# Linear-attention denominators: replicated by one matmul per group of heads, or made head-wise on 32-column array tiles and spread by DMA

## The chip, the cores and the metric

The kernel runs on one core of a Trainium2 chip. The time is the device time of one execution in microseconds, median over executions. All runs compared here are of the fast state (e6, a single look, counts as unknown), at a mean granted TensorE clock of 0.98 to 1.00, and each experiment ran beside the kernel before on the same chip. A profile is one execution; its span (first to last instruction) is 1.7 us shorter than its time (521.8 against 523.49 us before).

TensorE does the matmuls. VectorE, ScalarE and GpSimd are called DVE, ACT and POOL in the profile. SyncE (SP) issues nearly all DMA here; SPq is its sequencer. PEld is TensorE's weight load.

## The reference

For 2048 tokens of width 576 the kernel computes `x + attention(layernorm(x)) + geglu(layernorm(x))`. The attention is linear, with 32 heads of 18 columns:

```python
pq, pk = phi(q), phi(k)
kv = jnp.einsum("bhsd,bhse->bhde", pk, v)
z = jnp.einsum("bhsd->bhd", pk)
num = jnp.einsum("bhqd,bhde->bhqe", pq, kv)
den = jnp.einsum("bhqd,bhd->bhq", pq, z)[..., None] + 1e-6
o = num / den                      # one denominator per token and head
# ... then @ wo; and (gelu(x @ w_gate) * (x @ w_up)) @ w_down
```

## The kernel before

The 2048 tokens are worked in four chunks of 512. After an attention part at the start (to about 71 us), each token chunk has a gate/up phase of 18 blocks (matmuls on 64-row tiles in pairs) and a down phase of 4 token tiles with 2 half tiles each. A half tile is 36 matmuls of the down projection and 5 of the attention, summed in one PSUM bank (PSUM is the memory in which TensorE sums).

The features of the heads lie in five groups: four of 7 heads (126 rows) and one of 4 heads (72 rows). `pqT` holds the query features. The division is done by scaling `pqT` before the attention matmuls. The kernel before makes each denominator already replicated 18 times, with a block-masked `zrep` of 126 columns, so one matmul gives the denominators of one group in the layout of `pqT`:

```python
def den_mm(sc, c, bank):
    rows = DH * HCH[c]
    ps = ps_all[:rows, bank, :]
    nc.tensor.matmul(ps, lhsT=zrep[:rows, c, :rows], rhs=pqT[:rows, c, sc * SC:(sc + 1) * SC], start=True, stop=True)
    den_evac(sc, c, ps)               # VectorE: + eps, to SBUF
# ... den_norm: 128-column reciprocals on VectorE, then pqT *= d on GpSimd
# ... first token chunk: three row-paired units (12 matmuls) in gate/up blocks 2, 3 and 4
# ... later token chunks: one den_mm in each of 4 or 5 half tiles of the down phase before
```

Weights come three blocks ahead, on SP's queue, which waits for a free buffer (88.1 us in 67 waits in the profile before):

```python
if blk > 0:
    load_gu(blk + NWBUF - 1, i)       # NWBUF = 4, nc.sync.dma_start, waits until a buffer is free
```

And the two row tiles of a gate/up unit take turns on a bank through an empty instruction on another engine, GpSimd except in the very first block. That instruction stands in GpSimd's program order, so the second half of a unit waits for everything GpSimd has before it (1.39 us in e1 below):

```python
self.turn = self.relay.nop()          # relay: nc.gpsimd, or nc.sync for the first block
```

Of the kernel before, what the change touches and what calls it, by code (L numbers as in the profile page):

```python
# [39 lines left out]
TD = 4  # L40
XW = 640
PKW = 580


class _Ring:
# [11 lines left out]
def kernel(  # L57
# [68 lines left out]
    make_identity(nc, ident[:])  # L126
    eps_ln = const.tile([P, 1], F32, name="eps_ln")
    nc.vector.memset(eps_ln[:], EPS_LN)
    eps_att = const.tile([P, 1], F32, name="eps_att")
    nc.vector.memset(eps_att[:], EPS_ATT)  # L130

    def spin(count):

# [6 lines left out]
    pqT = persist.tile([P, NCH, S], BF16, name="pqT")  # L140
    wo2 = persist.tile([P, NCH, D], BF16, name="wo2")
    m_sb = persist.tile([P, NCH, D], BF16, name="m_sb")
    zrep = persist.tile([P, NCH, CR], BF16, name="zrep")
    kvT = persist.tile([P, NCH, CR], BF16, name="kvT")

    nc.vector.memset(pqT[HP:P, NCH - 1, 0:2 * SC], 0.0)
    nc.vector.memset(zrep[HP:P, NCH - 1, :], 0.0)

    def load_wo():
        nc.sync.dma_start(wo2[:CR, 0:4, :], A_wo[0:4 * CR, :].rearrange("(c p) j -> p c j", p=CR))  # L150
# [49 lines left out]
    nc.gpsimd.memset(g_sb[0:HP, 4, HALF:D], 0.0)  # L200
    nc.gpsimd.memset(g_sb[HP:P, 4, 0:HALF], 0.0)

    ZQ = 32
    z_ones = const.tile([P, ZQ], BF16, name="z_ones")
    nc.gpsimd.memset(z_ones[:], 1.0)
    z_sb = apool.tile([P, D], BF16, name="z_sb")
    nc.gpsimd.memset(z_sb[:], 0.0)
    zsel = const.tile([P, CR], BF16, name="zsel")
    nc.gpsimd.memset(zsel[:], 0.0)
    for g in range(P // ZQ):  # L210
        nc.gpsimd.memset(zsel[g * ZQ:g * ZQ + 1, :], 1.0)
# [249 lines left out]
        rows = DH * HCH[c]  # L461
        return ps_all[:rows, b4, c * CR:c * CR + rows] if c < 4 else ps_all[:rows, b1, 0:rows]

    def z_stage(b4, b1):
        for c in range(NCH):
            rows = DH * HCH[c]
            nc.tensor.matmul(
                chunk_out(c, b4, b1), lhsT=z_sb[:, c * CR:c * CR + rows], rhs=zsel[:, :rows],
                start=(c in (0, 4)), stop=True, skip_group_check=True,
            )  # L470
        mask_pair(zrep, b4, b1)

    def kv_stage(b4, b1):
        for kt in range(KT):
# [6 lines left out]
                )  # L481
        mask_pair(kvT, b4, b1)

    den_sb = {}

    def den_evac(sc, c, ps):
        rows = DH * HCH[c]
        d = dwork.tile([P, SC], F32, name="den_sb", tag="den_sb", bufs=6)
        nc.vector.tensor_scalar_add(out=d[:rows, :], in0=ps, scalar1=EPS_ATT)
        den_sb[sc, c] = d  # L490

    def den_mm(sc, c, bank):
        rows = DH * HCH[c]
        ps = ps_all[:rows, bank, :]
        nc.tensor.matmul(ps, lhsT=zrep[:rows, c, :rows], rhs=pqT[:rows, c, sc * SC:(sc + 1) * SC], start=True, stop=True)  # L495
        den_evac(sc, c, ps)

    def den_pair(items, outs):

        rows = DH * HCH[items[0][1]]  # L500

        def part(r):

            return slice(r.start, min(r.stop, P if rows <= P - HP + 8 else rows))

        return _Unit(
            outs,
            lambda i, r, kt: zrep[part(r), items[i][1], :rows],
            lambda i, r, kt: pqT[part(r), items[i][1], items[i][0] * SC:(items[i][0] + 1) * SC],
            nc.sync, first=(0,), then=(0,),  # L510
        )

    def den_norm(sc, c, q, pieces):
        w = SC // pieces
        rows = DH * HCH[c]
        d = den_sb[sc, c][:rows, q * w:(q + 1) * w]
        cols = slice(sc * SC + q * w, sc * SC + (q + 1) * w)
        for h in range(0, w, P):
            nc.vector.reciprocal(out=d[:, h:h + P], in_=d[:, h:h + P])  # L519

        def scale():
            nc.gpsimd.tensor_tensor(out=pqT[:rows, c, cols], in0=pqT[:rows, c, cols], in1=d, op=ALU.mult)  # L522
        return scale



# [84 lines left out]
    g_copy(1, (3, 288), [(ALL, 3, 0, 288, 288, nc.scalar), (ALL, 2, 0, 0, 288, nc.vector)])  # L611
    for _, step, n in todo[tail:]:
        step(n)
    q_unit(12)
    for step in (q_exp1, q_min, q_max):
        step(12)
    g_last(0)
    z_sums(1)
    g_copy(3, (6, 288), [(ALL, 6, 0, 288, 288, nc.scalar), (ALL, 5, 0, 0, 288, nc.vector)])
    g_copy(4, (0, 288), [(HI, 0, 0, 288, 288, nc.scalar), (LO, 0, 0, 0, 288, nc.vector)])  # L620
    z_copies(1)
    q_unit(13)
    z_stage(2, 3)
    kv_stage(6, 5)
    for step in (q_exp1, q_min, q_max):
        step(13)


    q_banks = _Ring(list(range(6)))
    prev = None  # L630
    for units in [[15, 16], [17, 18], [14, 19], None]:
        if units:
            u = q_pair(units)
            u.p1()
        if prev:
            prev[1].p2()
            for step in (q_exp1, q_min, q_max):
                for i in prev[0]:
                    step(i)
        prev = (units, u)  # L640
    scales = []
    den_jobs = [(0, c, q, 2) for c in range(NCH) for q in range(2)]

    asmall_cm.__exit__(None, None, None)
    awork_cm.__exit__(None, None, None)
# [9 lines left out]
            nc.sync.dma_start(wd_sb[:, f0:f0 + WDS, :], wd_view[:, f0:f0 + WDS, :])  # L655
            wd_loaded[0] += WDS


    DEN_FROM = 2
    DEN_PAIRS = [[(0, 0), (0, 1)], [(0, 2), (0, 3)], [(0, 4), (1, 4)]]  # L660

    def gu_pair(sc, k):
        cs = slice(sc * SC, (sc + 1) * SC)
        blk = sc * (NF // GUB) + k
        wg, wu, wr = gu_blocks.pop(blk)
        units = []
        for i in range(GUB):
            b = [banks.next(), banks.next()]
            fcol = slice(i * P, (i + 1) * P)

            def lhs(a, rows, kt, fcol=fcol):
                if kt == 4:
                    return wr[rows, fcol]
                return (wg, wu)[a][rows, kt, fcol]

            u = _Unit([ps_all[:, b[0], :], ps_all[:, b[1], :]], lhs, lambda a, rows, kt: xnT[rows, kt, cs],
                      nc.sync if blk == 0 else nc.gpsimd)
            if blk > 0:
                load_gu(blk + NWBUF - 1, i)
            u.p1()  # L680
            units.append((b, u))
        if sc == 0 and k == 1:
            load_wo()
        elif sc == 0 and k >= 2:
            load_wd_slice()
        den = None
        if sc == 0 and 0 <= k - DEN_FROM < len(DEN_PAIRS):
            items = DEN_PAIRS[k - DEN_FROM]
            den = den_pair(items, [ps_all[:DH * HCH[c], banks.next(), :] for _, c in items])
            den.p1()  # L690
        for i, (b, u) in enumerate(units):
            u.p2()
            gl = fwork.tile([P, SC], F32, name="gl")
            nc.scalar.activation(out=gl[:], in_=ps_all[:, b[0], :], func=ACT.Gelu_apprx_tanh)  # L694
            nc.vector.tensor_tensor(out=hT[:, GUB * k + i, :], in0=ps_all[:, b[1], :], in1=gl[:], op=ALU.mult)  # L695
        if den:
            den.p2()
            for (dsc, c), ps in zip(items, den.outs):
                den_evac(dsc, c, ps)

    def m_stage(c, acc_bank):
        rows = DH * HCH[c]
        for hf in range(2):
            b = (acc_bank + 2 + (2 * c + hf) % 6) % 8
            hs = slice(hf * HALF, (hf + 1) * HALF)
            nc.tensor.matmul(  # L706
                ps_all[:rows, b, :HALF], lhsT=kvT[:rows, c, :rows], rhs=wo2[:rows, c, hs], start=True, stop=True,
            )
            nc.scalar.copy(out=m_sb[:rows, c, hs], in_=ps_all[:rows, b, :HALF])

    def down_tile(sc, j, hooks):
        n = sc * TPC + j
# [3 lines left out]
        for hf in range(2):  # L716
            hs = slice(hf * HALF, (hf + 1) * HALF)
            todo = hooks.pop(0) if hooks else {}
            acc_bank = banks.next()
            acc = ps_all[:, acc_bank, :HALF]  # L720
            for f in range(NF):
                if f in todo:
                    todo[f](acc_bank)
                nc.tensor.matmul(  # L724
                    acc, lhsT=hT[:, f, j * P:(j + 1) * P], rhs=wd_sb[:, f, hs], start=(f == 0), stop=False,
                )
            for c in range(NCH):
                rows = DH * HCH[c]
                nc.tensor.matmul(  # L729
                    acc, lhsT=pqT[:rows, c, ts_], rhs=m_sb[:rows, c, hs], start=False, stop=(c == NCH - 1),  # L730
                )
            nc.vector.tensor_tensor(out=res[:, hs], in0=acc, in1=x_sb[:, n, hs], op=ALU.add)  # L732
            if last:
                nc.sync.dma_start(out_view[:, n, hs], res[:, hs])
        if not last:
            nc.sync.dma_start(out_view[:, n, :], res[:])

    for sc in range(NSC):
        for k in range(NF // GUB):
            gu_pair(sc, k)  # L740
            if scales:
                scales.pop(0)()
            if den_jobs and k > DEN_FROM:
                scales.append(den_norm(*den_jobs.pop(0)))
        while wd_loaded[0] < NF:
            load_wd_slice()

        hooks = [{6 * c_: (lambda b, c_=c_: m_stage(c_, b)) for c_ in range(NCH)} if sc == 0 else {}]
        if sc + 1 < NSC:
            for c_ in range(NCH):  # L750
                def dn(b, c=c_, nsc=sc + 1):
                    if (nsc, c) not in den_sb:
                        den_mm(nsc, c, (b + 2) % 8)
                    den_norm(nsc, c, 0, 1)()
                hooks.append({0: dn})
        for j in range(TPC):
            down_tile(sc, j, hooks)

# [29 lines left out]
```

## Time and profile before

| | before |
|---|---|
| time, median of the first 3 runs | 524.03 us (523.87 to 524.6) |
| span of the profiled run | 521.8 us |
| TensorE busy | 516.3 us |
| VectorE busy | 251.2 us, of which reciprocals 68.3 |
| a gate/up phase without denominators | 70.03 us (18 blocks of 3.89) |
| down phases 1 to 3, with denominators | 42.5, 41.4, 41.4 us |

The row of a group on the profile's page reads: line, engine and operation, tiles, shapes, count, then busy us and the mean ns of one, then the engine's idle time ahead of them and what ended it. These two rows are the work that the change shrinks and moves:

```profile
L519 DVE RECIPROCAL den_sb<-den_sb 126x128 f32<-126x128 f32 (+1 forms) x80 | 68.3, 910 | 0.5
...
L522 POOL TENSOR_TENSOR pqT<-pqT,den_sb 126x512 bf16<-126x512 bf16 (+3 forms) x25 | 24.1, 965 | 317.0 <-DVE den_sb L519 282.4
```

GpSimd's 317 us of idle time cost nothing: it is not on the chain that ended last, of which TensorE is 96%.

### The profile page before, as it was taken

The page shows a single profiled execution, that of the slowest core. Times are in us where ns is not written, and L with a number is a line of the kernel's source. Part 1 is how long each engine was busy: PE and PEld are TensorE (multiplying, and loading weights), DVE is VectorE, ACT ScalarE, POOL GpSimd, SP SyncE. Part 2 cuts the span into 40 slices and gives each one's busy share as a digit, 9 for nine tenths or more (in the row PEclk, how much of TensorE's full clock was granted, in tenths as well). Part 3 has the DMA queues.
Part 4 walks back from the last instruction along what each step waited for, and adds up shares of the span by engine and source line. Part 5 has one row for each costly group of instructions (what it writes and reads, how often), then busy time and mean ns, then how long its engine had stood idle before and what let it go on. Part 6 is the DMA issues. An engine that isn't in the chain of part 4 may idle for free.

```text
span 521.8 us, 10779 instructions
## 1 busy us (share of the span) xinstructions
PE 516.3 (99%) x4562; PEld 313.8 (60%) x4562; DVE 251.2 (48%) x438; ACT 143.8 (28%) x296; POOL 36.4 (7%) x62
## 2 busy tenths in 40 slices
PE   8999999999999999999999999999999999999997
PEld 7777755555587754444577644444777544445775
DVE  7996565876358323433388033333584233333100
ACT  6899442322320013323200032332000123322000
POOL 3011000211001100000012000000011000000000
PEclk9999999999999999999999999999999999999999
DMA  8434509898500045455300155555000355540000
GB/s 267 75 62 122 155 27 264 238 287 258 162 13 13 11 126 158 142 159 157 92 13 13 43 163 152 158 147 157 26 25 13 105 159 158 142 133 1 13 13 23
DMA packets 106362, 57.96 MB, mean 111 GB/s; under 512 B 13386, under 2 KB 105802, under 8 KB 106314
## 3 DMA queue, kind: packets, MB, share of 16 engines
q1 hardware_dynamic: 105706, 56.62, 38.8%
q8 instruction: 35, 0.57, 0.5%
q10 hardware_dynamic: 608, 0.66, 0.4%
q14 instruction: 13, 0.11, 0.1%
HBM read 52.94 MB, written 2.36 MB: 106 GB/s over the span
## 4 chain that ended last, share of the span: by engine, by line
PE 96%; ACT 1%; DMA 1%; DVE 1%; issue 0%; ACTq 0%
PE ps_all L358 55%; PE ps_all L724 27%; PE ps_all L729 4%; PE ps_all L259 3%; PE ps_all L303 3%; PE ps_all L387 3%; DMA wqkv_sb<-in_A_wqkv_dram 1%; PE ps_all L495 1%; PE ps_all L477 0%; PE ps_all L706 0%; ACT xnT L248 0%; ACT L116 0%; DVE g_sb L597 0%; ACT phi_e L279 0%; ACT z_sb L335 0%; DVE pqT L447 0%
## 5 line engine op out<-in xcount | busy, mean ns | idle before, releaser
L358 PE MATMUL ps_all<-xnT,wg 64*128 64x512 bf16 x1152 | 272.7, 376 | 0.0
L358 PE MATMUL ps_all<-xnT,wu 64*128 64x512 bf16 x1152 | 271.8, 376 | 0.0
L695 DVE TENSOR_TENSOR hT<-ps_all,gl 128x512 bf16<-128x512 f32 x144 | 99.4, 691 | 162.0 <-ACT gl L694 161.3
L694 ACT ACTIVATE gl<-ps_all 128x512 f32<-128x512 f32 x144 | 86.0, 597 | 314.4 <-PE ps_all L358 295.0
L358 PEld LDWEIGHTS <-wu 64*128 64x128 bf16 x1152 | 108.3, 94 | 66.2
L358 PEld LDWEIGHTS <-wg 64*128 64x128 bf16 x1152 | 108.3, 94 | 66.0
L724 PE MATMUL ps_all<-wd_sb,hT 128*128 128x288 bf16 x1152 | 147.0, 286 | 0.0
L724 PEld LDWEIGHTS <-hT 128*128 128x128 bf16 x1152 | 112.3, 98 | 30.7 <-issue 1.3
L519 DVE RECIPROCAL den_sb<-den_sb 126x128 f32<-126x128 f32 (+1 forms) x80 | 68.3, 910 | 0.5
L732 DVE TENSOR_TENSOR res<-ps_all,x_sb 128x288 bf16<-128x288 f32 x32 | 14.6, 457 | 88.0 <-PE ps_all L729 88.0
L358 PE MATMUL ps_all<-xnT,wr 64*128 64x512 bf16 x288 | 55.2, 376 | 0.0
L522 POOL TENSOR_TENSOR pqT<-pqT,den_sb 126x512 bf16<-126x512 bf16 (+3 forms) x25 | 24.1, 965 | 317.0 <-DVE den_sb L519 282.4
L729 PE MATMUL ps_all<-m_sb,pqT 126*128 126x288 bf16 (+1 forms) x160 | 24.9, 286 | 0.0
L358 PEld LDWEIGHTS <-wr 64*128 64x128 bf16 x288 | 14.5, 94 | 16.8 <-issue 0.7
L259 PE MATMUL ps_all<-wqkv_sb,xnT 128*128 128x288 bf16 x160 | 22.5, 286 | 0.6 <-DMA wqkv_sb<-in_A_wqkv_dram 0.5
L259 PEld LDWEIGHTS <-xnT 128*128 128x128 bf16 x160 | 15.3, 98 | 6.7 <-issue 0.8
L303 PE MATMUL ps_all<-hT,xn 128*128 128x288 bf16 (+4 forms) x144 | 18.2, 273 | 0.0
L729 PEld LDWEIGHTS <-pqT 126*128 126x128 bf16 (+1 forms) x160 | 15.5, 97 | 4.1
L387 PE MATMUL ps_all<-xnT,wqkv_sb 128*126 128x512 bf16 (+1 forms) x70 | 17.4, 379 | 0.0
L303 PEld LDWEIGHTS <-xn 128*128 128x128 bf16 x144 | 13.9, 98 | 3.3
L287 DVE SCALAR_TENSOR_TENSOR hT<-ps_all,phi_e 128x288 bf16<-128x288 f32 x32 | 13.2, 449 | 4.4 <-ACT phi_e L283 3.8
L279 ACT ACTIVATE phi_e<-ps_all 128x288 f32<-128x288 f32 x32 | 12.9, 409 | 3.4 <-PE ps_all L259 1.9
(78 smaller groups left out, 184.7 us busy)
## 6 DMA issues: line engine op xcount, KB each, us to landing
wg<-in_B_w_gate_dram SPq DMA_DIRECT2D x72, 256.0 KB, 2.8
wu<-in_B_w_up_dram SPq DMA_DIRECT2D x72, 256.0 KB, 3.5
wd_sb<-in_B_w_down_dram SPq DMA_DIRECT2D x12, 432.0 KB, 4.5
wr<-in_B_w_gate_dram SPq DMA_DIRECT2D x72, 32.0 KB, 2.6
wr<-in_B_w_up_dram SPq DMA_DIRECT2D x72, 32.0 KB, 3.0
out_dram<-res SPq DMA_DIRECT2D x15, 144.0 KB, 1.8
x_sb<-in_A_x_dram SPq DMA_DIRECT2D x3, 576.0 KB, 7.4
wqkv_sb<-in_A_wqkv_dram SPq DMA_DIRECT2D x2, 576.0 KB
```

The source lines that it names most:

```text
L259: nc.tensor.matmul(ps_all[:, k_bank(n, hf), :HALF], lhsT=xnT[:, kt, n * P:(n + 1) * P], rhs=wqkv_sb[:, kt, D + hf * HALF:D + (hf + 1) * HALF],
L287: nc.vector.scalar_tensor_tensor(out=out_, in0=ps, scalar=0.0, in1=e, op0=ALU.max, op1=ALU.add)
L303: nc.tensor.matmul(ps_all[:, b, col:col + w], lhsT=xn[:, n, kt * P:(kt + 1) * P], rhs=pk[:, n, p0:p0 + w], start=(n == 0 and col == 0), st ...
L358: return nc.tensor.matmul(self.outs[i], lhsT=self.lhs(i, rows, kt), rhs=self.rhs(i, rows, kt), start=start, stop=stop, skip_group_check=True,)
L387: nc.tensor.matmul(ps, lhsT=wqkv_sb[:, kt, q0:q0 + rows], rhs=xnT[:, kt, sc * SC:(sc + 1) * SC], start=(kt == 0), stop=(kt == KT - 1),)
L519: nc.vector.reciprocal(out=d[:, h:h + P], in_=d[:, h:h + P])
L522: nc.gpsimd.tensor_tensor(out=pqT[:rows, c, cols], in0=pqT[:rows, c, cols], in1=d, op=ALU.mult)
L694: nc.scalar.activation(out=gl[:], in_=ps_all[:, b[0], :], func=ACT.Gelu_apprx_tanh)
L695: nc.vector.tensor_tensor(out=hT[:, GUB * k + i, :], in0=ps_all[:, b[1], :], in1=gl[:], op=ALU.mult)
L724: nc.tensor.matmul(acc, lhsT=hT[:, f, j * P:(j + 1) * P], rhs=wd_sb[:, f, hs], start=(f == 0), stop=False,)
L729: nc.tensor.matmul(acc, lhsT=pqT[:rows, c, ts_], rhs=m_sb[:rows, c, hs], start=False, stop=(c == NCH - 1),)
L732: nc.vector.tensor_tensor(out=res[:, hs], in0=acc, in1=x_sb[:, n, hs], op=ALU.add)
```

## The change

Its intent is to spend less of TensorE on denominators. Instead of 18 copies of each, one row per head is computed: 7 heads fit a 32-column tile, and four groups are to run at once on four column tiles. VectorE then has 16 reciprocals instead of 80. The replication moves to DMA: each head's row of 512 numbers (one SBUF partition) is copied to 18 partitions, and GpSimd scales `pqT` as before. This copying is called the spread below. In the first token chunk it is issued at block 14, behind the last weights of that chunk, and the attention sums of a half tile come after the next half tile's down matmuls. Query units 12 and 13 become a row-paired unit, and the hand-over (the last stage of the attention part, from the Gram matmuls, which sum key features times normalized tokens, to the first gate/up block) is reordered. The core of the diff, cut:

```diff
-        mask_pair(zrep, b4, b1)
+        nc.vector.tensor_tensor(
+            out=zden[:CR, 0:4, 0:7], in0=ps_all[:CR, b, 0:4 * ZQ].rearrange("p (c h) -> p c h", c=4)[:, :, 0:7],
+            in1=heads[:CR].unsqueeze(1).to_broadcast([CR, 4, 7]), op=ALU.mult,
+        )
 ... (the fifth group: columns Z4 = 8 to 11 of its own tile)
+    def den_mm(sc, bank):
+        for g in range(4):
+            nc.tensor.matmul(
+                ps_all[g * ZQ:(g + 1) * ZQ, bank, :], lhsT=zden[:CR, g, :], rhs=pqT[:CR, g, sc * SC:(sc + 1) * SC],
+                start=True, stop=False, skip_group_check=True,
+            )
 ... (four 128-column matmuls for the fifth group, one in each column tile)
+    def den_spread(sc, c):
+        d = den_sb[sc]
 ... (den_rep: one buffer of [P, NCH, SC] F32)
+        if c < 4:
+            parts = [(c * ZQ, 0, SC)]
+        else:
+            parts = [(g * ZQ + Z4, g * TQ, TQ) for g in range(4)]
+        for p0, t0, w in parts:
+            nc.sync.dma_start(
+                to[:rows, c, t0:t0 + w],
+                d[p0:p0 + nh, t0:t0 + w].unsqueeze(1).to_broadcast([nh, DH, w]),
+            )
 ...
-    for units in [[15, 16], [17, 18], [14, 19], None]:
+    for units in [[12, 13], [15, 16], [17, 18], [14, 19], None]:
 ...
+            open_halves.append(attention)
+            end = sc == 0 and not (j == TPC - 1 and hf == 1)
+            while len(open_halves) > end:
+                open_halves.pop(0)()
 ...
+        den_jobs[NF // GUB - NWBUF].append(lambda c=c: den_spread(0, c))
+        den_jobs[NF // GUB - 1].append(lambda c=c: den_scale(0, c))
```

For later token chunks the spread is issued one half tile into the down phase before, and the scaling follows two half tiles later.

More of the change, by code (lines that the diff above doesn't have):

```diff
@@ L42 @@
 PKW = 580
+ZQ = 32
+Z4 = 8
 class _Ring:
@@ L128 @@
     nc.vector.memset(eps_ln[:], EPS_LN)
-    eps_att = const.tile([P, 1], F32, name="eps_att")
-    nc.vector.memset(eps_att[:], EPS_ATT)
     def spin(count):
@@ L142 @@
     m_sb = persist.tile([P, NCH, D], BF16, name="m_sb")
-    zrep = persist.tile([P, NCH, CR], BF16, name="zrep")
+    zden = persist.tile([P, NCH, ZQ], BF16, name="zden")
     kvT = persist.tile([P, NCH, CR], BF16, name="kvT")
-    nc.vector.memset(pqT[HP:P, NCH - 1, 0:2 * SC], 0.0)
-    nc.vector.memset(zrep[HP:P, NCH - 1, :], 0.0)
+    nc.gpsimd.memset(zden[:], 0.0)
     def load_wo():
@@ L201 @@
     nc.gpsimd.memset(g_sb[HP:P, 4, 0:HALF], 0.0)
-    ZQ = 32
     z_ones = const.tile([P, ZQ], BF16, name="z_ones")
@@ L207 @@
     nc.gpsimd.memset(z_sb[:], 0.0)
-    zsel = const.tile([P, CR], BF16, name="zsel")
+    zsel = const.tile([P, ZQ], BF16, name="zsel")
     nc.gpsimd.memset(zsel[:], 0.0)
@@ L462, in chunk_out, with z_stage @@
         return ps_all[:rows, b4, c * CR:c * CR + rows] if c < 4 else ps_all[:rows, b1, 0:rows]
-    def z_stage(b4, b1):
+    def z_stage(b):
         for c in range(NCH):
@@ L467, in z_stage @@
             nc.tensor.matmul(
-                chunk_out(c, b4, b1), lhsT=z_sb[:, c * CR:c * CR + rows], rhs=zsel[:, :rows],
-                start=(c in (0, 4)), stop=True, skip_group_check=True,
-            )
-        mask_pair(zrep, b4, b1)
+                ps_all[:rows, b, c * ZQ:(c + 1) * ZQ], lhsT=z_sb[:, c * CR:c * CR + rows], rhs=zsel[:],
+                start=(c == 0), stop=True, skip_group_check=True,
+            )
+        heads = bmask[:].rearrange("p (h e) -> p h e", e=DH)[:, :, 0]
+        nc.vector.tensor_tensor(
+            out=zden[:CR, 0:4, 0:7], in0=ps_all[:CR, b, 0:4 * ZQ].rearrange("p (c h) -> p c h", c=4)[:, :, 0:7],
+            in1=heads[:CR].unsqueeze(1).to_broadcast([CR, 4, 7]), op=ALU.mult,
+        )
+        r4 = DH * HCH[4]
+        nc.vector.tensor_tensor(
+            out=zden[:r4, 4, Z4:Z4 + HCH[4]], in0=ps_all[:r4, b, 4 * ZQ:4 * ZQ + HCH[4]],
+            in1=heads[:r4, 0:HCH[4]], op=ALU.mult,
+        )
     def kv_stage(b4, b1):
@@ L482, in kv_stage @@
         mask_pair(kvT, b4, b1)
-    den_sb = {}
-    def den_evac(sc, c, ps):
-        rows = DH * HCH[c]
-        d = dwork.tile([P, SC], F32, name="den_sb", tag="den_sb", bufs=6)
-        nc.vector.tensor_scalar_add(out=d[:rows, :], in0=ps, scalar1=EPS_ATT)
-        den_sb[sc, c] = d
-    def den_mm(sc, c, bank):
-        rows = DH * HCH[c]
-        ps = ps_all[:rows, bank, :]
-        nc.tensor.matmul(ps, lhsT=zrep[:rows, c, :rows], rhs=pqT[:rows, c, sc * SC:(sc + 1) * SC], start=True, stop=True)
-        den_evac(sc, c, ps)
@@ L498, in den_pair @@
-    def den_pair(items, outs):
-        rows = DH * HCH[items[0][1]]
-        def part(r):
-            return slice(r.start, min(r.stop, P if rows <= P - HP + 8 else rows))
-        return _Unit(
-            outs,
-            lambda i, r, kt: zrep[part(r), items[i][1], :rows],
-            lambda i, r, kt: pqT[part(r), items[i][1], items[i][0] * SC:(items[i][0] + 1) * SC],
-            nc.sync, first=(0,), then=(0,),
-        )
-    def den_norm(sc, c, q, pieces):
-        w = SC // pieces
-        rows = DH * HCH[c]
-        d = den_sb[sc, c][:rows, q * w:(q + 1) * w]
-        cols = slice(sc * SC + q * w, sc * SC + (q + 1) * w)
-        for h in range(0, w, P):
-            nc.vector.reciprocal(out=d[:, h:h + P], in_=d[:, h:h + P])
-        def scale():
-            nc.gpsimd.tensor_tensor(out=pqT[:rows, c, cols], in0=pqT[:rows, c, cols], in1=d, op=ALU.mult)
-        return scale
+    den_sb, den_rep = {}, {}
@@ new lines @@
+    TQ = SC // 4
+    def den_mm(sc, bank):
[4 more added lines that the diff above has]
+            )
+        r4 = DH * HCH[4]
+        for g in range(4):
+            t0 = sc * SC + g * TQ
+            nc.tensor.matmul(
+                ps_all[g * ZQ:(g + 1) * ZQ, bank, g * TQ:(g + 1) * TQ], lhsT=zden[:r4, 4, :],
+                rhs=pqT[:r4, 4, t0:t0 + TQ], start=False, stop=True, skip_group_check=True,
+            )
@@ new lines, in den_evac, with den_recip @@
+    def den_evac(sc, bank):
+        d = dwork.tile([P, SC], F32, name="den_sb", tag="den_sb", bufs=2)
+        nc.vector.tensor_scalar_add(out=d[:], in0=ps_all[:, bank, :], scalar1=EPS_ATT)
+        den_sb[sc] = d
+    def den_recip(sc, q):
+        d = den_sb[sc][:, q * P:(q + 1) * P]
+        nc.vector.reciprocal(out=d, in_=d)
+    def den_spread(sc, c):
+        d = den_sb[sc]
+        if sc not in den_rep:
+            den_rep[sc] = dwork.tile([P, NCH, SC], F32, name="den_rep", tag="den_rep", bufs=1)
+        to = den_rep[sc]
+        nh = HCH[c]
+        rows = DH * nh
+        if c < 4:
[6 more added lines that the diff above has]
+                d[p0:p0 + nh, t0:t0 + w].unsqueeze(1).to_broadcast([nh, DH, w]),
+            )
@@ L528, with den_scale @@
+    def den_scale(sc, c):
+        rows = DH * HCH[c]
+        cols = slice(sc * SC, (sc + 1) * SC)
+        nc.gpsimd.tensor_tensor(
+            out=pqT[:rows, c, cols], in0=pqT[:rows, c, cols], in1=den_rep[sc][:rows, c, :], op=ALU.mult,
+        )
     TILE = 2.94
@@ L613 @@
         step(n)
-    q_unit(12)
-    for step in (q_exp1, q_min, q_max):
-        step(12)
+    z_sums(1)
     g_last(0)
-    z_sums(1)
     g_copy(3, (6, 288), [(ALL, 6, 0, 288, 288, nc.scalar), (ALL, 5, 0, 0, 288, nc.vector)])
+    z_copies(1)
     g_copy(4, (0, 288), [(HI, 0, 0, 288, 288, nc.scalar), (LO, 0, 0, 0, 288, nc.vector)])
-    z_copies(1)
-    q_unit(13)
-    z_stage(2, 3)
-    kv_stage(6, 5)
-    for step in (q_exp1, q_min, q_max):
-        step(13)
-    q_banks = _Ring(list(range(6)))
+    z_stage(2)
+    kv_stage(4, 5)
+    for sc, bank in ((0, 3), (1, 2)):
+        den_mm(sc, bank)
+        den_evac(sc, bank)
+    q_banks = _Ring([6, 7, 0, 1, 2, 3, 4, 5])
     prev = None
-    for units in [[15, 16], [17, 18], [14, 19], None]:
+    for units in [[12, 13], [15, 16], [17, 18], [14, 19], None]:
         if units:
@@ L640 @@
         prev = (units, u)
-    scales = []
-    den_jobs = [(0, c, q, 2) for c in range(NCH) for q in range(2)]
     asmall_cm.__exit__(None, None, None)
@@ L656, in load_wd_slice @@
             wd_loaded[0] += WDS
-    DEN_FROM = 2
-    DEN_PAIRS = [[(0, 0), (0, 1)], [(0, 2), (0, 3)], [(0, 4), (1, 4)]]
     def gu_pair(sc, k):
@@ L685, in gu_pair @@
             load_wd_slice()
-        den = None
-        if sc == 0 and 0 <= k - DEN_FROM < len(DEN_PAIRS):
-            items = DEN_PAIRS[k - DEN_FROM]
-            den = den_pair(items, [ps_all[:DH * HCH[c], banks.next(), :] for _, c in items])
-            den.p1()
         for i, (b, u) in enumerate(units):
@@ L695, in gu_pair @@
             nc.vector.tensor_tensor(out=hT[:, GUB * k + i, :], in0=ps_all[:, b[1], :], in1=gl[:], op=ALU.mult)
-        if den:
-            den.p2()
-            for (dsc, c), ps in zip(items, den.outs):
-                den_evac(dsc, c, ps)
     def m_stage(c, acc_bank):
@@ L709, in m_stage @@
             nc.scalar.copy(out=m_sb[:rows, c, hs], in_=ps_all[:rows, b, :HALF])
+    open_halves = []
     def down_tile(sc, j, hooks):
@@ L725, in down_tile, with attention @@
                     acc, lhsT=hT[:, f, j * P:(j + 1) * P], rhs=wd_sb[:, f, hs], start=(f == 0), stop=False,
+                    skip_group_check=True,
                 )
-            for c in range(NCH):
-                rows = DH * HCH[c]
-                nc.tensor.matmul(
-                    acc, lhsT=pqT[:rows, c, ts_], rhs=m_sb[:rows, c, hs], start=False, stop=(c == NCH - 1),
-                )
-            nc.vector.tensor_tensor(out=res[:, hs], in0=acc, in1=x_sb[:, n, hs], op=ALU.add)
-            if last:
-                nc.sync.dma_start(out_view[:, n, hs], res[:, hs])
-        if not last:
-            nc.sync.dma_start(out_view[:, n, :], res[:])
+            def attention(hf=hf, hs=hs, acc=acc):
+                for c in range(NCH):
+                    rows = DH * HCH[c]
+                    nc.tensor.matmul(
+                        acc, lhsT=pqT[:rows, c, ts_], rhs=m_sb[:rows, c, hs], start=False, stop=(c == NCH - 1),
+                        skip_group_check=True,
+                    )
+                nc.vector.tensor_tensor(out=res[:, hs], in0=acc, in1=x_sb[:, n, hs], op=ALU.add)
+                if last:
+                    nc.sync.dma_start(out_view[:, n, hs], res[:, hs])
+                elif hf == 1:
+                    nc.sync.dma_start(out_view[:, n, :], res[:])
+            open_halves.append(attention)
+            end = sc == 0 and not (j == TPC - 1 and hf == 1)
+            while len(open_halves) > end:
+                open_halves.pop(0)()
+    den_jobs = {k: [] for k in range(NF // GUB)}
+    for q in range(4):
+        den_jobs[2 + q].append(lambda q=q: den_recip(0, q))
+        den_jobs[6 + q].append(lambda q=q: den_recip(1, q))
+    for c in range(NCH):
+        den_jobs[NF // GUB - NWBUF].append(lambda c=c: den_spread(0, c))
+        den_jobs[NF // GUB - 1].append(lambda c=c: den_scale(0, c))
     for sc in range(NSC):
@@ L740 @@
             gu_pair(sc, k)
-            if scales:
-                scales.pop(0)()
-            if den_jobs and k > DEN_FROM:
-                scales.append(den_norm(*den_jobs.pop(0)))
+            for job in den_jobs.pop(k, ()):
+                job()
         while wd_loaded[0] < NF:
             load_wd_slice()
-        hooks = [{6 * c_: (lambda b, c_=c_: m_stage(c_, b)) for c_ in range(NCH)} if sc == 0 else {}]
+        hooks = [{} for _ in range(2 * TPC)]
+        if sc == 0:
+            hooks[0] = {6 * c_: (lambda b, c_=c_: m_stage(c_, b)) for c_ in range(NCH)}
+        jobs = [[] for _ in range(2 * TPC)]
         if sc + 1 < NSC:
-            for c_ in range(NCH):
-                def dn(b, c=c_, nsc=sc + 1):
-                    if (nsc, c) not in den_sb:
-                        den_mm(nsc, c, (b + 2) % 8)
-                    den_norm(nsc, c, 0, 1)()
-                hooks.append({0: dn})
+            for c in range(NCH):
+                jobs[1].append(lambda b, c=c, n=sc + 1: den_spread(n, c))
+                jobs[3 + c].append(lambda b, c=c, n=sc + 1: den_scale(n, c))
+        if sc + 2 < NSC:
+            jobs[2].append(lambda b, n=sc + 2: (den_mm(n, (b + 2) % 8), den_evac(n, (b + 2) % 8)))
+            for q in range(4):
+                jobs[3 + q].append(lambda b, q=q, n=sc + 2: den_recip(n, q))
+        for todo, js in zip(hooks, jobs):
+            if js:
+                todo[0] = lambda b, js=js: [job(b) for job in js]
         for j in range(TPC):
```

## The prediction

> **What bounds the kernel now.** I read the page's busy line and chain first, then stretches around the places where the change acts, then single instructions.
>
> ```profile
> PE 516.3 (99%) x4562; PEld 313.8 (60%) x4562; DVE 251.2 (48%) x438; ACT 143.8 (28%) x296; POOL 36.4 (7%) x62
> ...
> PE 96%; ACT 1%; DMA 1%; DVE 1%; issue 0%; ACTq 0%
> ```
>
> TensorE is busy for 516.3 of 521.8 us and is 96% of the chain that ended last; VectorE is half idle. So only what shortens TensorE's stream counts. The 68 us of reciprocals that the change takes from VectorE (80 x 910 ns) are not on that chain, and are worth nothing by themselves.
>
> The stretches of the first gate/up chunk, one block each (engines PE, PEld, DVE, ACT, POOL, then clock, DMA share, GB/s):
>
> ```profile
> 75.20:79.09 3.89, 3.89 (x40) 1.75 (x36) 1.50 (x3) 1.20 (x3) 0.00 (x0) 1.00 0.48 130
> 79.09:83.40 4.31, 4.31 (x44) 2.07 (x40) 1.53 (x3) 1.23 (x3) 0.00 (x0) 1.00 0.95 253
> 83.40:87.70 4.30, 4.30 (x44) 2.23 (x40) 2.55 (x5) 1.19 (x2) 0.00 (x0) 1.00 1.01 297
> 87.70:92.03 4.33, 4.33 (x44) 2.34 (x41) 4.16 (x7) 1.19 (x2) 0.00 (x0) 1.00 0.91 251
> 92.03:95.92 3.89, 3.89 (x40) 2.07 (x37) 3.77 (x6) 1.09 (x2) 0.67 (x1) 1.00 0.83 244
> ```
>
> A plain block takes 3.89 us, the three with a pair of denominator units 4.31, 4.30 and 4.33. The clock is full. DMA is nearly saturated here: a rival below rests on that.
>
> In the down phase the timeline has, for a half tile with a denominator matmul and for one without:
>
> ```profile
> 158.94 0.78 PE L729 MATMUL ps_all<-m_sb,pqT 126*128 126x288 bf16 x5
> 159.56 0.38 PE L495 MATMUL ps_all<-pqT,zrep 126*126 126x512 bf16 x1
> 159.78 4.57 PE L724 MATMUL ps_all<-wd_sb,hT 128*128 128x288 bf16 x36
> 164.19 0.78 PE L729 MATMUL ps_all<-m_sb,pqT 126*128 126x288 bf16 x5
> ...
> 174.46 0.78 PE L729 MATMUL ps_all<-m_sb,pqT 126*128 126x288 bf16 x5
> 175.08 4.57 PE L724 MATMUL ps_all<-wd_sb,hT 128*128 128x288 bf16 x36
> 179.49 0.78 PE L729 MATMUL ps_all<-m_sb,pqT 126*128 126x288 bf16 x5
> ```
>
> From one attention group's start to the next: 5.25 us with it, 5.03 without, so one denominator costs 0.22 us (159.56 to 159.78). Its shown 0.38 includes latency that the next matmul overlaps; I therefore count start to start.
>
> The hand-over from attention to gate/up, where the change reorders most:
>
> ```profile
> 57.59 1.24 PE L387 MATMUL ps_all<-xnT,wqkv_sb 128*126 128x512 bf16 x5
> 58.76 2.17 PE L312 MATMUL ps_all<-hT,xn 128*64 128x289 bf16 x32
> 60.86 1.20 PE L325 MATMUL ps_all<-hT,z_ones 128*32 128x144 bf16 x64
> 61.98 1.29 PE L387 MATMUL ps_all<-xnT,wqkv_sb 128*126 128x512 bf16 x5
> 63.11 1.07 PE L467 MATMUL ps_all<-zsel,z_sb 128*126 128x126 bf16 x5
> 64.02 1.59 PE L477 MATMUL ps_all<-g_sb,wqkv_sb 128*126 128x126 bf16 x25
> 65.54 0.43 PE L358 MATMUL ps_all<-xnT,wqkv_sb 64*126 64x512 bf16 x1
> ```
>
> The steps are 1.17, 2.10, 1.12, 1.13, 0.91 and 1.52 us; row-paired query work runs from 65.54 to 71.41. The 0.91 us for five small z matmuls is mostly a wait: the chain of waits leaves TensorE there and goes through VectorE and ScalarE from 58.87 to 63.88.
>
> [...] 64 sums of 144 columns take 1.12 us start to start[...]; and 16 pairs of 289 columns need about 1.98 us at the 123 ns that a 288-column matmul has here (4.41 us / 36) while the next phase starts 2.10 us later, so a mode change costs about 0.12 us.[...]
>
> **The change part by part.**
> *Removed.* Six paired steps in the first gate/up chunk: 4.31 + 4.30 + 4.33 - 3 x 3.89 = 1.27 us. Fourteen single matmuls in the down phases (4 + 5 + 5) at 0.215: 3.0 us. Together 4.3 us of TensorE.
> *Added.* Four head-wise groups, one per chunk: four column tiles of 512 columns at once (0.215, as any 512-column matmul here) and four of 128 columns at once (about 0.06): 0.275 us. The two in the down phases stand among full-array matmuls and pay two mode changes: 0.275 + 0.24 = 0.51 each, 1.0 us. The two at the hand-over share one extra mode change: 0.67 us.
> *Hand-over.* z sums 1.12[...], last Gram block 2.10, z matmuls 5 x 0.0625 = 0.31, kv 1.52, denominators 0.67, then four query pairs of nine steps at 0.216: 7.8. That sums to 13.6 us, against 71.41 - 57.59 = 13.8 before: query units 12 and 13 cost 1.95 as a pair instead of 2.2, and the wait of the z stage goes, which pays for the denominators. I checked that no new wait enters: the z copies take 1.43 us in a row (62.39 to 63.82 before) and now lie under the 2.1 us of the Gram block; its own copies (about 1.3 us with their serial ScalarE and VectorE halves) end near 62.3, while kv first needs them at 62.5; the small head masks follow by 62.7, and the first denominator matmul wants them at 62.8. These are margins of 0.1 to 0.2 us, so I keep only 0.1 us of the 0.2.
> *Moved off the path.* Scaling on GpSimd (5 x 1.16 us per chunk) and the spread. In the first chunk the spread is issued after block 17's weights, near 127.5;[...]. Block 17 ends near 141; GpSimd then scales until about 146.5. The first attention sums, put off by half a tile, come near 151.5: 5 us to spare. Without the delay they would come at 147, with almost none. In later chunks a spread has two half tiles (10 us) before its first scale.
> Sum: -1.27 - 3.0 + 1.0 - 0.1 = -3.4 us, so 524.0 - 3.4 = 520.6; I put 520.7.
>
> **The rivals.**
> *The hand-over becomes a wait.* For it: the margins of 0.1 to 0.2 us, and VectorE then has kv masks, two evictions (0.68 each) and four query pairs, each 2 us of VectorE against 1.94 of TensorE. Banks 4 and 5 must be free for block 1's second unit near 76.4; I get VectorE done with them near 75.8. Against it: before, it finished at 75.4 with the same bank needed at 76.2, and nothing stalled. If it happens: +0.3 to 1 us, 521 to 521.7.
> *The spread collides with the weights.* For it: DMA shares of 0.83 to 1.01 in blocks 2 to 6[...]. Against it: it comes after the last down weights, behind the last weights that this chunk needs; the following loads are for the next chunk, over 40 us later. Only a spread several times slower than estimated would hold up the first chunk's scaling and attention: at 15 us of movement the scaling ends after 152 and TensorE waits 1 to 5 us, so 522 to 526.
> *Column tiles do not pack at 512 columns.* If the four ran in turn, a group would cost 4 x 0.275 = 1.1 us, 0.8 more, times four: 3.3 us and no gain, 524. Against it: the z sums pack fully with 128 rows and different moving data for each tile.
> *It was VectorE all along.* A large gain would need VectorE's reciprocals on the path. TensorE shows no idle time before gate/up or down matmuls, so I give this almost nothing.
>
> **Range and chances.** A gain of 3.4 us is 0.65%. The upside is bounded by the 4.3 us removed plus about 0.7 of hand-over wait[...]; the likely downside is a new wait of up to 1.5 us. The range is 519.7 to 522.3. A gain over 2% needs 10.5 us, more than twice all removed work: 0.01. A loss over 2% needs a spread that stalls TensorE by 14 us: 0.02. Within 2%: 0.97.
>
> **What would show it.** The blocks of 4.3 us fall to 3.89. In each down phase with denominators, one half tile is longer by about 0.5 us instead of four or five by 0.22, and the third chunk's has none. The four column matmuls start within a few tens of ns of each other. The first gate/up block starts within 0.3 us of 71.4. The first spread has landed by 140, and GpSimd's scaling ends before the first delayed attention group. TensorE's busy time falls by about 3.4 us with its share still 99%. I would be wrong if TensorE shows idle time before a query pair, block 1 or the first attention group, or if a head-wise group takes about 1 us.

The sum: -1.27 - 3.0 + 1.0 - 0.1 = -3.4 us, so 520.6, put as 520.7. One term is inside the hand-over's 13.6 us: 0.1 us more for going over to the z sums. The 0.12 us for a mode change (from one tile shape to another) is an estimate from the trace before (2.10 us to the next phase, of which the matmuls need about 1.98); why it costs that is not shown. The 0.0625 us of a z matmul is an estimate too: the z sums' 1.12 us less that 0.12, over 16 steps of four sums. That the spread would land before 140 was my estimate: no trace of before has such a transfer.

## The result, and the profile after

| | before | after |
|---|---|---|
| time, median (4 runs each) | 524.01 us | 527.43 us (526.91 to 528.19) |
| span of the profiled run | 521.8 us | 525.5 us |

The ratio is 1.0064 (95% interval 1.0047 to 1.0082). A ratio here is the mean time of one kernel's fast runs over that of the other's of the same rounds, so it is not quite the ratio of the medians quoted. The kernel became slower by 0.6%, outside the predicted range.

The busy line and the chain of waits after:

```profile
PE 515.0 (98%) x4576; PEld 307.9 (59%) x4576; DVE 187.2 (36%) x355; ACT 143.7 (27%) x296; POOL 35.2 (7%) x58
...
PE 91%; SPq 5%; DMA 2%; ACT 1%; POOL 0%; DVE 0%; issue 0%; POOLq 0%
```

TensorE fell from 96% of the chain to 91%. In its place stands above all SyncE's sequencer (5%), which was not on the chain before, and DMA rises from 1% to 2%: something waits for a transfer, and the transfer's issue.

First what went as planned. A stretch of the first gate/up phase in which a block of 4.33 us used to lie:

```profile
87.98:91.87 3.89, 3.89 (x39) 1.75 (x36) 2.25 (x4) 1.20 (x3) 0.00 (x0) 1.00 1.10 300
```

The length of this window was chosen, so it proves only that TensorE is never idle in it, with 39 matmuls recorded (40 in a plain block before, 44 in one with denominators). The measure is the whole phase: 70.02 us, as long as a phase without denominators (70.03).

A head-wise group in the second down phase, on TensorE's timeline:

```profile
270.17 0.78 PE L736 MATMUL ps_all<-m_sb,pqT 126*128 126x288 bf16 x5
270.88 0.40 PE L498 MATMUL ps_all<-pqT,zden 126*32 126x512 bf16 x4
271.10 0.23 PE L505 MATMUL ps_all<-pqT,zden 72*32 72x128 bf16 x4
271.26 4.58 PE L728 MATMUL ps_all<-wd_sb,hT 128*128 128x288 bf16 x36
275.69 0.78 PE L736 MATMUL ps_all<-m_sb,pqT 126*128 126x288 bf16 x5
```

Four matmuls of 512 columns occupy 0.22 us (270.88 to 271.10), as one did before. From attention group to attention group it is 5.52 us, 0.49 more than the plain 5.03.

The hand-over, where new waits were feared:

```profile
58.50 1.19 PE L323 MATMUL ps_all<-hT,z_ones 128*32 128x144 bf16 x64
...
61.72 0.44 PE L465 MATMUL ps_all<-zsel,z_sb 128*126 128x32 bf16 x5
62.01 1.59 PE L484 MATMUL ps_all<-g_sb,wqkv_sb 128*126 128x126 bf16 x25
63.53 0.40 PE L498 MATMUL ps_all<-pqT,zden 126*32 126x512 bf16 x4
```

The z stage takes 0.29 us instead of 0.91 and no row carries an idle note. From the start of the Gram matmuls to the first gate/up matmul it was 52.87 to 71.41, 18.54 us; it is now 53.68 to 72.01, 18.33 us.

Then where the time went, in the first down phase. In square brackets stands the idle time ahead of an instruction, and what ended it:

```profile
152.15 0.53 PE L736 MATMUL ps_all<-m_sb,pqT 126*128 126x288 bf16 x3
154.67 0.30 PE L736 MATMUL ps_all<-m_sb,pqT 126*128 126x288 bf16 x1 [1.99 <-POOL pqT L540]
157.72 0.42 PE L736 MATMUL ps_all<-m_sb,pqT 72*128 72x288 bf16 x1 [2.75 <-POOL pqT L540]
...
158.73 5.64 PE L728 MATMUL ps_all<-wd_sb,hT 128*128 128x288 bf16 x36
```

The first attention group comes half a tile late, as designed, and still waits twice, 4.74 us, for GpSimd's scaling. After that, 36 down matmuls take 5.6 us instead of 4.6. The clock column (third from the end) says why:

```profile
158.80:164.40 5.60, 5.60 (x38) 4.11 (x39) 0.69 (x1) 0.00 (x0) 0.00 (x0) 0.81 0.78 214
164.40:169.40 5.00, 5.00 (x43) 3.98 (x42) 1.32 (x2) 0.00 (x0) 0.00 (x0) 1.00 0.40 49
```

The mean granted clock was 0.81 in the half tile after the wait, then 1.00 again. (The record behind it has 0.50 from 157.52 to 160.93 us and 1.00 before and after.) The chain of waits shows what GpSimd waited for:

```profile
128.81 0.96 SPq L532
129.82 0.80 SPq L532
130.66 4.63 SPq L532
135.33 4.09 SPq L532
...
150.82 5.53 DMA den_rep<-den_sb
156.51 1.17 POOL pqT L540
```

Line 532 is the spread. Its first two issues take under a microsecond (0.96 and 0.80), as the weight loads just ahead of them do (0.37 to 0.59), the next five 3.3 to 4.6 us each and the last one 2.1. It looks as if the sequencer is held back by what the earlier ones have not finished; the experiments bear this out, where the same eight issues get shorter as the transfers get faster (24.1 us at 49 GB/s, 12.9 at 99, 8.2 at 176). The eight issues take from 128.81 to 152.93, and the last piece lands at 156.4. The prediction had it landed by 140.

The differences by phase add up to the loss (spans): start of the kernel +0.81, hand-over -0.21, first gate/up 71.34 to 70.02, -1.32, first down phase 42.48 to 48.65, +6.17, second 41.42 to 40.82, -0.60, third 41.43 to 40.33, -1.10. The sum is +3.75, the spans differ by 3.77. The start is a load: TensorE's first projection waited for it until 7.26 us before and 8.07 after. Over the nine profiles of the experiments below, whose start is the same as the changed kernel's or nearly so, that moment lies anywhere from 7.01 to 8.12. So it is scatter of a load between executions, not an effect of the change.

### The profile page after: what moved, and what is told of

The parts are those of the page before. It is cut to its first block, busy times and chain, and to the rows that moved or that the text cites. A ratio compares the mean times of both kernels' runs of the same rounds, so it can differ in the third digit from the quotient of the medians.

```text
span 525.5 us, 10760 instructions
## 1 busy us (share of the span) xinstructions
PE 515.0 (98%) x4576; PEld 307.9 (59%) x4576; DVE 187.2 (36%) x355; ACT 143.7 (27%) x296; POOL 35.2 (7%) x58
## 4 chain that ended last, share of the span: by engine, by line
PE 91%; SPq 5%; DMA 2%; ACT 1%; POOL 0%; DVE 0%; issue 0%; POOLq 0%
PE ps_all L356 52%; PE ps_all L728 25%; SPq L532 4%; PE ps_all L736 4%; PE ps_all L257 3%; PE ps_all L301 3%; PE ps_all L385 2%; DMA wqkv_sb<-in_A_wqkv_dram 1%; DMA den_rep<-den_sb 1%; PE ps_all L310 0%; PE ps_all L484 0%; PE ps_all L498 0%; POOL pqT L540 0%; ACT xnT L246 0%; ACT L118 0%; PE ps_all L323 0%
## 5 line engine op out<-in xcount | busy, mean ns | idle before, releaser
L540 POOL TENSOR_TENSOR pqT<-pqT,den_rep 126x512 bf16<-126x512 bf16 (+1 forms) x20 | 23.2, 1159 | 317.4 <-DMA den_rep<-den_sb 235.2
L517 DVE RECIPROCAL den_sb<-den_sb 128x128 f32<-128x128 f32 x16 | 15.1, 942 | 0.0
L385 PE MATMUL ps_all<-xnT,wqkv_sb 128*126 128x512 bf16 (+1 forms) x60 | 14.9, 378 | 0.0
L277 ACT ACTIVATE phi_e<-ps_all 128x288 f32<-128x288 f32 x32 | 12.9, 409 | 4.0 <-PE ps_all L257 2.6
```

Of the source, the lines that this page charges most:

```text
L385: nc.tensor.matmul(ps, lhsT=wqkv_sb[:, kt, q0:q0 + rows], rhs=xnT[:, kt, sc * SC:(sc + 1) * SC], start=(kt == 0), stop=(kt == KT - 1),)
L517: nc.vector.reciprocal(out=d, in_=d)
L540: nc.gpsimd.tensor_tensor(out=pqT[:rows, c, cols], in0=pqT[:rows, c, cols], in1=den_rep[sc][:rows, c, :], op=ALU.mult,)
```

## The experiments

All started from the changed kernel, and each ran beside the kernel before on the same chip. The theory was: the whole loss is TensorE waiting for a slow spread, and the lowered clock after it. The rivals for why the spread is slow were: few DMA engines at work (the busy share is 0.40; from 132 to 136 us the trace never has more than seven of its 2 KB packets in flight at once), a fixed cost per row, slow issue by the queue whatever the transfer, or the place of the source rows. The last was at first only my supposition: neither kernel's trace shows it, and e5, e6 and e9 were made to test it.

The DMA share of 0.43 in e5's and e6's texts is that of the change (0.40 from 132 to 136 us, 0.44 from 127 to 158).

**e1: attention two half tiles late.** The slow spread stays, and the wait is moved out of its reach.

```diff
-            end = sc == 0 and not (j == TPC - 1 and hf == 1)
+            end = 2 if sc == 0 and not (j == TPC - 1 and hf == 1) else 0
```

> Edit: in the first chunk the attention sums come two half tiles late instead of one; the slow spread stays. Theory A (the whole loss is TensorE waiting 4.7 us for the first chunk's spread, plus about 1.5 us of lowered clock after the wait): the wait vanishes, TensorE idles under 0.5 us there, the clock stays at 1.00, and the time falls by about 6 us from 527.4 to 521.2. Theory B (something else in the changed kernel costs time, such as mode changes or the hand-over): at most the 4.7 us go and the time stays above 522.5. The spread still takes about 24 us of issue in both.

Measured: 523.76 us (522.69 to 527.62, 4 runs), ratio 1.0025 (0.9981 to 1.0069): by the time alone this is what theory B had forecast (above 522.5), and A's 521.2 was missed. The slowest of the four runs was as slow as the change, and no trace of it was kept. In the profiled run (523.23 us) the wait at the attention group did go: the trace has no idle time there. But another appeared at the next gate/up phase, and this execution also began late:

```profile
188.71 0.39 PE L356 MATMUL ps_all<-xnT,wu 64*128 64x512 bf16 x1 [1.39 <-POOLq L365]
```

```profile
7.99 1.36 PE L257 MATMUL ps_all<-wqkv_sb,xnT 128*128 128x288 bf16 x5 [1.49 <-DMA wqkv_sb<-in_A_wqkv_dram]
```

Line 365 is the empty relay instruction on GpSimd. The second token chunk's spread is as slow as the first (24 us of issue), so GpSimd's last scaling waits for it and starts only at 188.65, in the change at 189.41. The relay stands behind it in GpSimd's order. In the change, gate/up began so late (190.68) that this did not show; once TensorE is some 5 us earlier, it meets this second effect of the same slowness. Against e3 below, the fastest run (span 517.9 against 521.5), e1 loses 1.9 us before the first down phase begins (all of it in the first 14.2 us, at the start, where times scatter) and 1.6 us at the relay (186.94 to 188.71, less the usual 0.22): 3.5 of the 3.6 us, so almost nothing is left for theory B in this trace. It supports theory A with one wait more than I had counted. What settles it are e3 and e5 below: they keep the changed kernel's mode changes and hand-over and speed up the spread alone, and the loss is gone.

**e3: half the bytes.** Reciprocals written and spread as bf16.

```diff
-            den_rep[sc] = dwork.tile([P, NCH, SC], F32, name="den_rep", tag="den_rep", bufs=1)
+            den_rep[sc] = dwork.tile([P, NCH, SC], BF16, name="den_rep", tag="den_rep", bufs=1)
 ... (the reciprocal writes a bf16 tile, which is the spread's source)
```

> Edit: the reciprocals are written and spread in bf16, so each row is 1 KB instead of 2 KB; rows, engines and source partitions unchanged. If the spread's time goes by bytes[...]: issue falls from 24 to about 12 us, the first chunk's wait goes, 521.2 us. If it goes by rows (a fixed cost of about 230 ns each): 24 us again and about 527.4 us.

(230 ns is about the 4.1 us of one slow issue over the 18 copies of a row.)

Measured: 519.86 us, ratio 0.9933 (0.9918 to 0.9948), correct. The issue takes 13.7 us. So it goes mostly by bytes, not rows, and with the spread faster the loss is gone. The first down phase lasts 42.1 us at clock 1.00.

**e4: two rows per head.** The column of a head is doubled in the stationary tile, which costs TensorE nothing that shows (a head-wise group takes 0.39 us to the next matmul, 0.38 in the change); 14 rows, each copied 9 times. What follows the cut is expected if the number of engines at work or the place of the source rows is the limit.

```diff
-                d[p0:p0 + nh, t0:t0 + w].unsqueeze(1).to_broadcast([nh, DH, w]),
+                d[p0:p0 + NR * nh, t0:t0 + w].unsqueeze(1).to_broadcast([NR * nh, DH // NR, w]),
 ... (NR = 2; zden holds each head in two neighbouring columns, the fifth group from column 16)
```

> Edit: each head's denominator is made in two rows, by doubling its column in the stationary tile (free on TensorE), so a spread has 14 source rows, each copied 9 times. [...] issue 24 to about 12 us[...], no wait, 521.2 us. Theory of a fixed rate for such copies whatever the engines[...]: unchanged, 24 us and 527.4.

Measured: 520.33 us, ratio 0.9937 (0.9923 to 0.9952); issue 13.6 us. The DMA share below rises from 0.40 to 0.74, and each row gives half the bytes, so this agrees with either limit, engines or source rows, and rules out slow issue as such.

**e5: the same 7 rows, four partitions apart.** Rows, copies and bytes unchanged, only the place of the rows differs. What follows the cut is expected if that place is the limit; "two to three times" was my estimate.

```diff
-                d[p0:p0 + nh, t0:t0 + w].unsqueeze(1).to_broadcast([nh, DH, w]),
+                d[p0:p0 + HS * (nh - 1) + 1:HS, t0:t0 + w].unsqueeze(1).to_broadcast([nh, DH, w]),
 ... (HS = 4; zden holds head h in column 4h, the fifth group in 4h + 2)
```

> Edit: the seven heads' rows lie four partitions apart instead of next to each other; still 7 source rows[...], same bytes. Theory engines: nothing changes, 24 us of issue, DMA share 0.43, 527.4 us. [...] the spread gets two to three times faster, under 12 us, and the time is about 521.2 us.

Measured: 520.4 us, ratio 0.9944 (0.9929 to 0.996); issue 8.2 us, three times faster than the change with the same bytes and destinations at nearly the same DMA share (0.48 against 0.40). Engines were not the limit of the change; the place of the source rows was. The first attention group now comes without idle time:

```profile
152.19 0.78 PE L739 MATMUL ps_all<-m_sb,pqT 126*128 126x288 bf16 x5
```

**e6: two partitions apart.** The dose between (HS = 2, heads in columns 2h, the fifth group in 2h + 1). What follows [...] is expected if the distance of the rows sets the rate.

> Edit: the seven heads' rows lie two partitions apart (four apart in the earlier run, next to each other in the change). [...] the issue of a spread takes about half of 24 us, 11 to 13 us, between the 24 and the 8 us measured, with the DMA share still about 0.43. If only some other effect of a strided source made the run with rows four apart fast, this one should be at about 8 us too. Time near 520.4 either way.

Measured: 12.9 us of issue; one look, 520.4 us. It lies between the 24.1 and the 8.2, so it is not merely that any strided source is fast: the distance counts.

**e9: 14 rows, two apart.** Each row gives half the bytes of a row in e5 at half the distance (e4 with the two-apart placement). What follows the second cut is expected if the place of the rows is still the limit.

> Edit: two rows for each head (14 source rows[...]), and those rows two partitions apart[...], each copied 9 times. [...] nothing more is gained: issue about 8 us and 0.9 us each. If seven engines were the limit there: issue near 5 us. The kernel's time should be the same either way, about 520.3 us, 0.6 to 0.7% under the kernel before, since the spread is hidden in both; this is also the timed candidate for a version that beats both.

Measured: 520.4 us (520.14 to 521.66, 5 runs), ratio 0.9937 (0.9924 to 0.9951); issue 8.1 us. More engines busy than in e5 (a share of 0.72 against 0.48), the same bytes over the same stretch of partitions, and no faster. The issue time alone is a weak test here: eight of the shortest issues seen in e9 (0.69 us) already make 5.5 us, so the 5 us could hardly have shown. The rate below is the better sign, 179 GB/s against 176 in e5: the source rows still set it.

The stretch from 132 to 136 us, when only the spread moves, for the change, e3, e4, e6, e5 and e9 in this order. The last two columns are the mean busy share of the 16 DMA engines and GB/s:

```profile
132.00:136.00 4.00, 4.00 (x40) 1.85 (x38) 1.38 (x2) 1.19 (x2) 0.00 (x0) 1.00 0.40 49
```

```profile
132.00:136.00 4.00, 4.00 (x40) 1.84 (x38) 1.39 (x2) 1.19 (x2) 0.00 (x0) 1.00 0.34 59
```

```profile
132.00:136.00 4.00, 4.00 (x40) 1.85 (x38) 1.38 (x2) 1.19 (x2) 0.00 (x0) 1.00 0.74 112
```

```profile
132.00:136.00 4.00, 4.00 (x40) 1.79 (x38) 1.38 (x2) 1.20 (x2) 0.00 (x0) 1.00 0.42 99
```

```profile
132.00:136.00 4.00, 4.00 (x41) 1.81 (x38) 1.38 (x2) 1.19 (x2) 0.00 (x0) 1.00 0.48 176
```

```profile
132.00:136.00 4.00, 4.00 (x42) 1.76 (x38) 1.38 (x2) 1.20 (x2) 0.00 (x0) 1.00 0.72 179
```

The share follows the number of source rows (0.34 to 0.48 with 7 rows, 0.72 and 0.74 with 14), not how much is moved: at the same share of about 0.4 the rate is 49, 99 or 176 GB/s. What the rate and the issue time go with is how densely the source gives its bytes, counted for one group of seven heads (252 KB in f32) as the bytes of a row times its copies, over the partitions from one row to the next:

| run | rows | partitions from row to row | KB given by a row | KB per partition | DMA engines busy, share x 16 | issue of the first spread, us |
|---|---|---|---|---|---|---|
| change | 7 | 1 | 36 | 36 | 6.4 | 24.1 |
| e3, bf16 | 7 | 1 | 18 | 18 | 5.4 | 13.7 |
| e4, two rows | 14 | 1 | 18 | 18 | 11.8 | 13.6 |
| e6, two apart | 7 | 2 | 36 | 18 | 6.7 | 12.9 |
| e5, four apart | 7 | 4 | 36 | 9 | 7.7 | 8.2 |
| e9, both | 14 | 2 | 18 | 9 | 11.5 | 8.1 |

Equal KB per partition give equal times within 6%, whatever the busy engines, the rows' bytes or their distance. The rate can be read from the second spread too, in which GpSimd waits for each group; the change's scalings there:

```profile
170.44 1.16 POOL L540 TENSOR_TENSOR pqT<-pqT,den_rep 126x512 bf16<-126x512 bf16 x1 [12.78 <-DMA den_rep<-den_sb]
175.91 1.16 POOL L540 TENSOR_TENSOR pqT<-pqT,den_rep 126x512 bf16<-126x512 bf16 x1 [4.31 <-DMA den_rep<-den_sb]
181.93 1.16 POOL L540 TENSOR_TENSOR pqT<-pqT,den_rep 126x512 bf16<-126x512 bf16 x1 [4.86 <-DMA den_rep<-den_sb]
186.08 1.16 POOL L540 TENSOR_TENSOR pqT<-pqT,den_rep 126x512 bf16<-126x512 bf16 x1 [3.00 <-DMA den_rep<-den_sb]
```

They begin 5.5, 6.0 and 4.2 us apart, 5.2 in the mean, for 252 KB: about 50 GB/s. In e6 they are 2.6 to 2.8 us apart, about 95 GB/s. That agrees with the 49 and 99 GB/s of the stretches above. The runs test distances of one, two and four partitions within a group of heads; why neighbouring rows hold each other up, and how the groups act on each other, no run here tests.

**e2: attention sums in line again, slow spread.**

```diff
-            end = sc == 0 and not (j == TPC - 1 and hf == 1)
+            end = 0
```

> Edit: the changed kernel, with the first chunk's attention sums in line again (the half tile's delay undone); the slow spread stays. If the wait is set by when the scaling ends (157.7 in the changed kernel's trace), TensorE waits from about 147.5 to 157.7 instead of 4.7 us, with a lowered clock after it: about 5 us more than the change, 532 us. If the delay did nothing: 527.4.

Measured: 532.59 us, ratio 1.0165 (1.014 to 1.0189). TensorE waits 9.5 us in three pieces until 157.75, the same moment as in the change (157.72). The half tile's delay was worth about 5.2 us with the slow spread.

**e7: the same undoing on top of e5.**

> Edit: rows four partitions apart, and the half tile's delay undone. If the spread's rate was the whole fault, its scaling ends near 146.3 and the in-line attention sums come near 147.3, so the delay is worth nothing any more: about 520.4 us, within 0.5. If the delay matters by itself: 1 us more or above.

Measured: 520.8 us, ratio 0.9932 (0.9909 to 0.9955), and no wait at the attention group in the trace. With a fast spread the delay is worth nothing that shows.

**e8: the slow spread at block 6 instead of 14.**

```diff
-        den_jobs[NF // GUB - NWBUF].append(lambda c=c: den_spread(0, c))
+        den_jobs[6].append(lambda c=c: den_spread(0, c))
```

> Edit: the changed kernel, with the first chunk's spread issued at block 6 instead of block 14, slow as it is. The scaling is then done long before the attention sums, so the wait there goes (-6 us). But the spread blocks the issuing queue for about 24 us, while the weights are only three blocks (11.7 us) ahead: TensorE should wait about 12 us for block 10's weights, with a lowered clock after it: 534 to 538 us. If the queue's order does not matter (the weights are not held up): about 521 us.

Measured: 541.65 us, ratio 1.0332 (1.0311 to 1.0352); worse than expected. From the view of all waits, and the stretch from 129.3 us on:

```profile
PE ps_all L356 <- DMA wr<-in_B_w_gate_dram: 17.7, 1, 17.7
```

```profile
129.30:133.00 3.70, 3.14 (x16) 1.17 (x18) 0.00 (x0) 0.00 (x0) 0.00 (x0) 0.50 1.01 290
```

The spread holds SyncE's queue from 98.8 to 123.9, and block 10's weights, issued behind it, land only at about 128.4; TensorE idles 17.7 us until then and restarts at clock 0.50. I had counted the blocking against the prefetch of three blocks (25 less 12 us) but not the time for the late weights to arrive. The order in the queue matters, and putting the spread behind the last weights was right.

## Why the prediction was right or wrong

It was wrong: 520.7 us with a range of 519.7 to 522.3, against 527.43. By its steps:

1. *TensorE bounds the kernel, and VectorE's reciprocals are worth nothing.* Right. VectorE lost 64 us of work (251.2 to 187.2 busy), and the phases gained no more than the TensorE work taken from them.
2. *Six paired steps gone from gate/up, 1.27 us.* Right: 1.32.
3. *Fourteen matmuls gone from the down phases, two groups of 0.51 added.* Right: the group costs 0.49; the second down phase gained 0.60 (0.57 by the prediction's terms), the third 1.10 (1.075).
4. *Hand-over, 0.2 us worked out, 0.1 kept.* Right: 0.21 (on a slightly longer stretch, from the Gram matmuls on), and no new wait.
5. *The spread, landed by 140.* This is the step that failed. Its transfers took 24.1 us to issue and landed at 156.4. Its size was my estimate, which no trace had shown, and took no account of where the source rows lie. With the same rows four partitions apart (e5) the issue took 8.2 us, from 128.86 to 137.09.
6. *"5 us to spare" for the first attention sums.* Fell with step 5: scaling ended at 157.7 instead of 146.5, 4.74 us of waiting. The "two half tiles (10 us)" for the later spreads were too few for the same reason; in the change that cost nothing, since its late gate/up phase hid it, and in e1 it cost 1.6 us. The lowered clock adds about 1.3 us: 5.58 instead of 4.52 us for the 36 matmuls after a head-wise group, and 0.66 instead of 0.38 us for the group itself. Both together are 6.1 of the 6.5 us by which this down phase missed its predicted -0.35; the last 0.4 us I cannot assign. The slower clock is also one reason why TensorE's busy time fell by 1.3 us (516.3 to 515.0) and not by 3.4.
7. *The rival that the spread stalls the scaling.* It named the right wait, with 15 us of movement and 522 to 526 us as its result; it was given too small a weight, because the size of the spread rested on one figure, which no trace of this case shows. The cause in its name, weights in the way, was not it: the spread was slow while it moved alone. The other rivals did not occur.

With the spread repaired, the rest of the sum stands: 519.9 to 520.4 us in e3, e4, e5 and e9, against 520.6 worked out. These beat the kernel before by 0.6 to 0.7%, and the change too (527.43, though not run beside them). Which of the four is best the runs do not tell. e5 and e9 keep f32 and have the most slack (8.2 and 8.1 us of issue).

## What to carry to other kernels

When a DMA reads few rows many times, look at where they lie: the same 7 rows and 252 KB moved at 49 GB/s next to each other, 99 two partitions apart and 176 four apart; here the number of busy DMA engines said little about the rate (a share of 0.40, 0.42 and 0.48 in these three, 0.72 at 179 GB/s). A transfer issued in order on a queue also delays all that stands behind it there (17.7 us of TensorE in e8), and a wait of an engine that relays for another (GpSimd here) reaches that other engine (1.39 us in e1): give the slow transfer a place where nothing behind it is urgent. A size that decides a margin should not rest on one figure that no trace has shown.
